# Rows of w_out in pairs, columns of the first layer two apart, and w_in's tile by quarters

## The chip, the cores and the metric

The kernel runs on one core of a Trainium2 chip. The metric is device time in microseconds of one execution; the median of three runs is compared. A profile of one execution shows each instruction of each engine: TensorE (PE, with its weight loads as PEld), VectorE (DVE), ScalarE (ACT), GpSimd (POOL), SyncE (SP), and the DMA queues.

## The reference

Forgetting attention for 8 batches of 8 heads (576 positions, 64 values a head), then a two-layer perceptron with a tanh GELU over the 4608 rows of 512 values that the heads make together.

```python
def _attn_ref(q, k, v, f):
    scores = scale * q @ k.T
    cum = np.cumsum(np.log(np.clip(f, 0.0001, 1.0)), axis=-1)
    scores = np.where(causal, -1e9, scores + cum[..., :, None] - cum[..., None, :])
    attn = softmax(scores)
    return attn @ v

def _moe_ref(x, w_in, w_out):          # x: 4608 x 512, w_in: 512 x 2048, w_out: 2048 x 512
    h = x @ w_in
    g = 0.5 * h * (1.0 + np.tanh(c * (h + 0.044715 * h * h * h)))
    return g @ w_out
```

Inputs and output are float32; the kernel computes its matmuls in bfloat16.

## The kernel before

**Work.** Attention goes in 16 groups of four heads (`scores`, `mask`, `denominators`, `attn_out`), whose results land transposed in `xT` (the 512 model values on partitions in four tiles `dt`, the rows along the tile). The perceptron goes in 9 chunks of 512 rows. Its first layer multiplies `w_in_sb` (loaded as weights, 128 columns at a time, one tile `ft` of 16 of the 2048 hidden values) with a piece of `xT` that streams through; the result has hidden values on partitions, and ScalarE's GELU writes it to `gT`. The second layer loads pieces of `gT` as weights and streams `w_out_sb`.

**First layer, three forms.** `mlp_in_half` (L436) and `mlp_in` (L400) multiply plainly. `unit` (L484) and `two_units` (L536) take a quarter u of the hidden values (512 columns) in a scheme of seven products in place of eight. For it `w_blocks` cuts the quarter in four blocks a11, a12, a21, a22: the first and second pair of `dt`, by the first and second 256 columns. `w_in_sums` (L466, L468) makes sums of them. For k = 3 it writes a21 in place: `a21 = a11 - a21`. The second layer has a scheme of the same kind (`weight_sums`, `seven_products`).

**Weight loads with a stride, before.** `scores` loads `kT`, whose tile keeps two values side by side, as every second element along the tile; `attn_out` loads `vw` as every second of 64 columns.

**Loads.** `w_in` (4 MB) and `w_out` (4 MB) are float32 in memory and bfloat16 on chip, so they go through GpSimd's queue, like q and k, and the early loads of v. `load_w_in(c)` brings one of eight pieces: 2 KB rows of memory become 1 KB on chip, two to a partition. `load_w_out(c)` brings four tiles of 128 rows, a row of memory (2 KB) to a partition.

**Order.** All is written out by hand: tables of short words (`FRONT`, `SECOND`, `STEADY`, `FLUSH`, `LAST`) that `run` turns into instructions in that order on each engine. `WI.c` and `WO.c` are the loads; `J`, `I`, `Q` and `E` are parts of the first layer; `F` of the second; `UW.u.k` is step k of `w_in_sums` for quarter u on VectorE. The framework adds the waits between engines: it notes which parts of a tile an instruction reads and writes and lets later ones that overlap wait. The last table has this stretch, in which the steps of quarter 1 are made while TensorE runs products of quarter 2 and the second layer (`e.1.u.n` is the next n products of unit u for the last chunk):

```python
F.0.4 F.0.3 UW.1.3 e.1.2.1 UW.1.4 e.1.1.1 F.0.5 e.1.1.2 F.0.5
```

Of the kernel before, what the change touches and what calls it, by code (L numbers as in the profile page):

```python
# [9 lines left out]
BF16 = mybir.dt.bfloat16  # L10
# [6 lines left out]
def kernel(  # L17
# [10 lines left out]
    nc = tc.nc  # L28
# [10 lines left out]
    N_DT = D_MODEL // 128  # L39
# [97 lines left out]
    gT = singles.tile([128, N_FT, CH], BF16, name="gT")  # L137
    g1, g2, g4 = many(3, [128, HF, HC], BF16, "gsum")
    u1, u2, u4 = many(3, [128, HF, HD], BF16, "usum")
    w_in_sb = singles.tile([128, N_DT, D_FF], BF16, name="w_in_sb")  # L140
    xsum = many(4, [128, 2, HC], BF16, "xsum")
    wsum = {u: many(3, [128, 2, HC], BF16, f"wsum{u}_") for u in UNIT_LIST}
    w_out_sb = singles.tile([128, N_FT, D_MODEL], BF16, name="w_out_sb")
# [43 lines left out]
        return ins  # L187

    w_in_hbm = moe_w_in.rearrange("(u p x) n -> p u x n", p=128, x=2)
    w_out_hbm = moe_w_out.rearrange("(t p) n -> p t n", p=128)  # L190

    def load_w_in(c):
        u, n = c % 2, D_FF // 4
        s = slice(n * (c // 2), n * (c // 2 + 1))
        return nc.gpsimd.dma_start(out=w_in_sb[:, 2 * u:2 * u + 2, s], in_=w_in_hbm[:, u, :, s])

    def load_w_out(c):
        n = N_FT // 4
        return nc.gpsimd.dma_start(out=w_out_sb[:, n * c:n * (c + 1), :],
                            in_=w_out_hbm[:, n * c:n * (c + 1), :])  # L200

    parts = [(0, QA), (QA, S)]

# [183 lines left out]
    def mlp_in(c, pr, spare=False):  # L387

        n0 = CH * c % RING
        spans = [(n0, CH)] if n0 + CH <= RING else [(n0, HC), ((n0 + HC) % RING, HC)]  # L390
        if spare:
            ph = psO.tile([128, 1024], FP32, name="ps_h", tag="po").rearrange("p (a n) -> p a n", n=512)
        else:
            ph = psS.tile([128, 2, 512], FP32, name="ps_h", tag="s")
        for dts in (range(N_DT - 1), range(N_DT - 1, N_DT)):
            for j in range(2):
                ft = 2 * pr + j
                for dt in dts:
                    for n, (h0, cols) in enumerate(spans):
                        nc.tensor.matmul(  # L400
                            ph[:, j, n * cols:(n + 1) * cols],
                            w_in_sb[:, dt, 128 * ft:128 * ft + 128],
                            xT[:, dt, h0:h0 + cols],
                            start=(dt == 0 and n == 0), stop=(dt == N_DT - 1),
                            skip_group_check=True,
                        )
                    if dt == N_DT - 1 and j == 1:
                        nc.scalar.activation(gelus(c, 2 * pr, 2), ph, AF.Gelu_apprx_tanh)  # L408
                    yield
# [11 lines left out]
    def mlp_in_half(half, g, spare=False):  # L421

        if spare:
            ph = psO.tile([128, 1024], FP32, name="ps_h", tag="po").rearrange("p (a n) -> p a n", n=512)
        else:
            ph = psS.tile([128, 2, 512], FP32, name="ps_h", tag="s")
        n0 = QA * half
        at = [ph.rearrange("p a (b n) -> p (a b) n", n=QA)]
        later[half, g] = lambda: nc.scalar.activation(gT[:, 4 * g:4 * g + 4, n0:n0 + QA], at[0], AF.Gelu_apprx_tanh)
        held[half, g] = at  # L430
        cut = 2 if spare else N_DT - 1
        for dts in (range(cut), range(cut, N_DT)):
            for j in range(4):
                ft = 4 * g + j
                for dt in dts:
                    nc.tensor.matmul(  # L436
                        ph[:, j // 2, QA * (j % 2):QA * (j % 2) + QA],
                        w_in_sb[:, dt, 128 * ft:128 * ft + 128],
                        xT[:, dt, n0:n0 + QA],
                        start=(dt == 0 and j % 2 == 0), stop=(dt == N_DT - 1),  # L440
                        skip_group_check=True,
                    )
                    if not spare and j == 3 and dt == N_DT - 1:
                        later[half, g]()
                    yield
# [9 lines left out]
        eng.tensor_sub(*((t1, b12, b11), (t2, b22, t1), (t3, b22, b12), (t4, b21, t2))[k - 1])  # L455

    def w_blocks(u):
        f1, f2 = slice(512 * u, 512 * u + 256), slice(512 * u + 256, 512 * u + 512)
        return w_in_sb[:, 0:2, f1], w_in_sb[:, 2:4, f1], w_in_sb[:, 0:2, f2], w_in_sb[:, 2:4, f2]

    def w_in_sums(u, k, eng):

# [7 lines left out]
    def unit(c, u, spare):  # L470

        a11, a12, s3, a22 = w_blocks(u)
        s1, s2, s4 = wsum[u]
        t1, t2, t3, t4 = xsum
        if spare:
            pa, pb = (psS.tile([128, 2, 512], FP32, name="ps_u", tag="s")[:, 0, :].rearrange("p (n t) -> p n t", t=HC)
                      for _ in range(2))
        else:
            pa, pb = (psM.tile([128, 2, HC], FP32, name="ps_u", tag="m") for _ in range(2))

        def multiply(ps, w, x, first):
            for n in range(2):
                for d in range(2):
                    nc.tensor.matmul(ps[:, n, :], w[:, d, 128 * n:128 * n + 128], x[:, d, :],  # L484
                                     start=(first and n == 0 and d == 0), stop=(d == 1), skip_group_check=True)

        def keep(ps, eng):
            t = unit_pool.tile([128, 2, HC], FP32, name="usnap", tag="usnap")
            if eng is nc.scalar:
                eng.copy(t, ps)  # L490
            else:
                eng.tensor_copy(t, ps)
            return t

        def result(a, t, src):
            ft = 4 * u + 2 * a
            nc.scalar.activation(gelus(c, ft, 2)[:, :, HC * t:HC * t + HC], src, AF.Gelu_apprx_tanh)

        def sum_of(a, t, ps, kept):
            nc.vector.tensor_add(kept, ps, kept)  # L500
            result(a, t, kept)

        multiply(pa, a11, x_block(c, 0, 0), True)
        p1 = keep(pa, nc.scalar)
        yield
        multiply(pb, a12, x_block(c, 1, 0), True)
        sum_of(0, 0, pb, p1)
        yield
        multiply(pa, s2, t2, False)
        v2 = keep(pa, nc.scalar)  # L510
        yield
        multiply(pb, s3, t3, True)
        p7 = keep(pb, nc.scalar)
        yield
        multiply(pa, s1, t1, False)
        sum_of(1, 1, pa, p7)
        yield
        multiply(pb, a22, t4, False)
        sum_of(1, 0, pb, v2)
        yield  # L520
        multiply(pa, s4, x_block(c, 1, 1), False)
        result(0, 1, pa)
        yield

    def two_units(c):

        blocks = [w_blocks(u) + tuple(wsum[u]) for u in (0, 2)]
        t1, t2, t3, t4 = xsum
        pa, pb = (psS.tile([128, 2, 512], FP32, name="ps_q", tag="s") for _ in range(2))

        def multiply(ps, which, x, first):
            for k in range(2):
                w = blocks[k][which]
                for n in range(2):
                    for d in range(2):
                        nc.tensor.matmul(ps[:, k, HC * n:HC * n + HC], w[:, d, 128 * n:128 * n + 128], x[:, d, :],  # L536
                                         start=(first and n == 0 and d == 0), stop=(d == 1), skip_group_check=True)
                if k == 0:
                    yield

        def keep(ps):
            t = unit_pool.tile([128, 2, 512], FP32, name="usnap", tag="usnap")
            nc.scalar.copy(t, ps)
            return t

        def result(a, t, src):
            nc.scalar.activation(  # L547
                gT.rearrange("p (u f) n -> p u f n", f=4)[:, 0:3:2, 2 * a:2 * a + 2, HC * t:HC * t + HC],
                src.rearrange("p u (f n) -> p u f n", n=HC), AF.Gelu_apprx_tanh)

        def sum_of(a, t, ps, kept):
            nc.vector.tensor_add(kept, ps, kept)  # L552
            result(a, t, kept)

        A11, A12, S3, A22, S1, S2, S4 = range(7)
        yield from multiply(pa, A11, x_block(c, 0, 0), True)
        p1 = keep(pa)
        yield
        yield from multiply(pb, A12, x_block(c, 1, 0), True)
        sum_of(0, 0, pb, p1)  # L560
        yield
        yield from multiply(pa, S2, t2, False)
        v2 = keep(pa)
        yield
        yield from multiply(pb, S3, t3, True)
        p7 = keep(pb)
        yield
        yield from multiply(pa, S1, t1, False)
        sum_of(1, 1, pa, p7)
        yield  # L570
        yield from multiply(pb, A22, t4, False)
        sum_of(1, 0, pb, v2)
        yield
        yield from multiply(pa, S4, x_block(c, 1, 1), False)
        result(0, 1, pa)
        yield
# [312 lines left out]
```

## Time and profile before

| | |
|---|---|
| median of three runs | 322.18 us (321.74 to 322.78) |
| profiled execution | 322.02 us, span 320.1 us |
| granted TensorE clock, mean | 1.000 |
| TensorE matmuls, busy | 311.8 us (97%) |
| TensorE weight loads, busy | 219.1 us (68%) |
| VectorE, ScalarE, GpSimd, busy | 242.5, 212.9, 109.9 us |
| `w_in` loads | 8, issued from 6.7 to 19.6 us |
| `w_out` loads | 4, issued from 21.4 to 29.7 us |

The span is the time from the first to the last instruction; the profiled execution's own time has some 2 us around it. A row of a group names line, engine, operation, tiles (out<-in), shapes and count, then busy time and the mean of one in ns, then idle time of the engine before them. A row of a timeline has start and length in us. Busy time of matmuls overlaps from one to the next, so their distance from start to start counts, not their length.

### The profile page before, as it was taken

How to read it: one execution, taken by the hardware profiler on the slowest of the kernel's cores; microseconds unless marked ns; L12 is line 12 of the kernel's file. 1: busy time of each engine (PE TensorE's matmuls, PEld its weight loads, DVE VectorE, ACT ScalarE, POOL GpSimd, SP SyncE). 2: the span in 40 equal slices, each digit the busy share in tenths (PEclk: the TensorE clock that was granted, in tenths of full speed). 3: DMA queues.
4: the chain of work that ended last, by engine and by line, in shares of the span. 5: the costliest groups of instructions: out<-in, count | busy, mean ns of one | idle time of the engine just before them, and what ended most of it. 6: DMA issues, size and time to landing. Idle time of an engine off the chain costs nothing.

```text
span 320.1 us, 11762 instructions
## 1 busy us (share of the span) xinstructions
PE 311.8 (97%) x5301; PEld 219.1 (68%) x5318; DVE 242.5 (76%) x369; ACT 212.9 (67%) x246; POOL 109.9 (34%) x148
## 2 busy tenths in 40 slices
PE   6899999999999999999999999999999999999996
PEld 2367734545676577776788878767776786688785
DVE  7667528598878889879877987699876865597674
ACT  3766885966766876877677866787686744836610
POOL 8799541830340417311850075206610140000000
PEclk9999999999999999999999999999999999999999
DMA  7999999985253901693149411961011110100203
GB/s 127 227 197 204 208 222 223 171 153 105 51 99 100 215 9 39 137 190 72 39 97 218 84 39 44 218 137 38 5 60 40 35 39 33 35 33 2 100 33 99
DMA packets 47491, 33.41 MB, mean 104 GB/s; under 512 B 29777, under 2 KB 42193, under 8 KB 47441
## 3 DMA queue, kind: packets, MB, share of 16 engines
q0 software_dynamic: 9632, 15.99, 29.1%
q1 hardware_dynamic: 37664, 16.60, 19.4%
q8 instruction: 41, 0.67, 0.9%
q14 instruction: 10, 0.07, 0.1%
q10 hardware_dynamic: 144, 0.07, 0.1%
HBM read 36.85 MB, written 9.44 MB: 145 GB/s over the span
## 4 chain that ended last, share of the span: by engine, by line
PE 91%; DMA 3%; ACT 2%; POOL 1%; DVE 1%; issue 1%; DVEq 0%; POOLq 0%
PE ps_w L616 30%; PE ps_h L400 19%; PE po L352 9%; PE ps_s L282 9%; PE ps_q L536 8%; PE pso L685 5%; PE ps_h L436 5%; PE ps_u L484 4%; DMA v_nat<-in_v_dram 3%; PE po_m L338 1%; ACT gT L408 1%; ACT pt L290 1%; POOL v_nat L183 0%; PE ps_o L352 0%; PE ps_p L616 0%
## 5 line engine op out<-in xcount | busy, mean ns | idle before, releaser
L290 ACT ACTIVATE pt<-ps_s 128x1024 bf16<-128x1024 f32 (+2 forms) x100 | 94.2, 991 | 38.1 <-PE ps_s L282 36.4
L296 POOL TENSOR_SCALAR_AFFINE_SELECT pt<-pt 128x512 bf16<-128x512 bf16 (+3 forms) x73 | 46.2, 643 | 96.6 <-ACT pt L290 73.7
L400 PE MATMUL ps_h<-xT,w_in_sb 128*128 128x512 bf16 (+1 forms) x308 | 65.6, 357 | 1.1 <-issue 0.3
L400 PEld LDWEIGHTS <-w_in_sb 128*128 128x128 bf16 x320 | 31.2, 98 | 26.6 <-issue 0.6
L408 ACT ACTIVATE gT<-ps_h 128x1024 bf16<-128x1024 f32 x34 | 34.6, 1018 | 20.3 <-PE ps_h L400 20.0
L616 PEld LDWEIGHTS <-gT 128*32 128x32 bf16 (+1 forms) x1171 | 44.1, 97 | 5.8 <-issue 2.4
L616 PE MATMUL ps_w<-w_out_sb,gT 128*32 128x256 bf16 (+1 forms) x996 | 42.5, 273 | 0.0
L616 PEld LDWEIGHTS <-gsum 128*32 128x32 bf16 (+1 forms) x903 | 35.3, 97 | 4.0 <-issue 1.5
L282 PE MATMUL ps_s<-qT,kT 32*128 32x64 bf16 (+5 forms) x896 | 35.4, 261 | 0.9 <-DVE qT L213 0.6
L552 DVE TENSOR_TENSOR usnap<-ps_q,usnap 128x1024 f32<-128x1024 f32 x15 | 17.9, 1222 | 18.5 <-PE ps_q L536 13.2
L616 PE MATMUL ps_w<-usum,gsum 128*32 128x256 bf16 (+1 forms) x749 | 30.1, 273 | 0.0
L282 PEld LDWEIGHTS <-kT 32*128 32x128 bf16 x896 | 16.4, 92 | 17.2 <-issue 10.2
L230 POOL TENSOR_TENSOR vw<-v_nat,wT 128x1280 bf16<-128x1280 f32 (+1 forms) x12 | 27.3, 2275 | 1.4 <-DMA v_nat<-in_v_dram 1.1
L633 DVE COPY snap<-ps_w 128x512 f32<-128x512 f32 x32 | 21.8, 681 | 6.6 <-PE ps_w L616 6.5
L213 DVE STREAM_TRANSPOSE kT<-k_c 128x576 f32<-128x576 f32 x16 | 19.4, 1243 | 7.0 <-DMA k_c<-in_k_dram 7.0
L547 ACT ACTIVATE gT<-usnap 128x1024 bf16<-128x1024 f32 x15 | 15.8, 1054 | 12.1 <-DVE usnap L552 11.7
L384 DVE TENSOR_TENSOR xT<-po,rb 128x576 bf16<-128x576 f32 x26 | 19.5, 751 | 5.1 <-PE po L352 4.9
L213 DVE STREAM_TRANSPOSE qT<-q_c 128x576 f32<-128x576 f32 x16 | 19.7, 1241 | 3.7 <-DMA q_c<-in_q_dram 3.7
L352 PE MATMUL po<-pt,vw 128*32 128x64 bf16 (+4 forms) x624 | 22.4, 278 | 0.0
L206 POOL DMA_DIRECT2D k_c<-in_k_dram x16 | 9.1, 567 | 34.9 <-DVE kT L213 23.0
L352 PEld LDWEIGHTS <-vw 128*32 128x32 bf16 x672 | 14.6, 97 | 9.3 <-issue 2.6
L536 PEld LDWEIGHTS <-w_in_sb 128*128 128x128 bf16 x160 | 15.7, 98 | 2.5 <-issue 0.4
(134 smaller groups left out, 481.4 us busy)
## 6 DMA issues: line engine op xcount, KB each, us to landing
out_dram<-o_st SPq DMA_DIRECT2D x35, 256.0 KB, 2.2
k_c<-in_k_dram POOLq DMA_DIRECT2D x16, 288.0 KB, 5.6
q_c<-in_q_dram POOLq DMA_DIRECT2D x16, 288.0 KB, 6.1
v_nat<-in_v_dram SPq DMA_DIRECT2D x16, 256.0 KB, 5.3
v_nat<-in_v_dram SPq DMA_DIRECT2D x20, 128.0 KB, 5.2
v_nat<-in_v_dram POOLq DMA_DIRECT2D x8, 256.0 KB, 8.8
w_in_sb<-in_moe_w_in_dram POOLq DMA_DIRECT2D x8, 256.0 KB, 7.9
w_out_sb<-in_moe_w_out_dram POOLq DMA_DIRECT2D x4, 512.0 KB, 9.8
```

What stands on the lines that cost most here:

```text
L213: return nc.vector.transpose(out=dst.rearrange("p s c -> p (s c)").bitcast(FP32) .rearrange("p (t a) -> p a t", a=n), in_=src.rearrange("p ...
L230: return eng.tensor_mul(vw[i % 2][:, t0:t1], vb[:, t0:t1, h0:h0 + 4, :], wT[:, i, t0:t1, :].unsqueeze(3).to_broadcast([128, t1 - t0, 4, D]))
L282: nc.tensor.matmul(tiles[h // 2][:, h % 2, c0:c0 + nq], key_columns(i, key, h, c), qq[32 * h:32 * h + 32, q0:q0 + nq, c], start=(c == 0 an ...
L290: nc.scalar.activation(p[:, 2 * g:2 * g + 2, off:off + n], t[:, :, 0:n], AF.Exp, scale=scale)
L296: nc.gpsimd.affine_select(out=x, in_=x, compare_op=ALU.is_ge, fill=0.0, base=0, pattern=pattern, channel_multiplier=-1)
L352: nc.tensor.matmul(po[r0:r0 + w.shape[-1], 448 + q0:448 + q0 + nq], w, p[:, h, col:col + nq], start=(key in (0, "low")), stop=(key in ("lo ...
L384: nc.vector.tensor_mul(xT[:, 2 * u + x, r0 + s0:r0 + s1], po, rbs[i, part])
L400: nc.tensor.matmul(ph[:, j, n * cols:(n + 1) * cols], w_in_sb[:, dt, 128 * ft:128 * ft + 128], xT[:, dt, h0:h0 + cols], start=(dt == 0 and ...
L408: nc.scalar.activation(gelus(c, 2 * pr, 2), ph, AF.Gelu_apprx_tanh)
L536: nc.tensor.matmul(ps[:, k, HC * n:HC * n + HC], w[:, d, 128 * n:128 * n + 128], x[:, d, :], start=(first and n == 0 and d == 0), stop=(d ...
L616: nc.tensor.matmul(ps[c0:c0 + width, n, cols[0]:cols[1]], x[:, j, 128 * n + c0:128 * n + c0 + width], w[:, j, cols[0]:cols[1]], start=(fir ...
L633: copy(kept[name], ps)
```

## The change

`w_out_hbm` is cut so that a partition takes two neighbouring rows of memory (4 KB, which are 2 KB on chip): tile 2t + x, partition p, now holds row 256t + 2p + x. So that the hidden values of `gT` stand on the same partitions, the first layer takes the columns of `w_in_sb` two apart: tile ft is every second column, from the odd or the even one, of a block of 256 (`ff_tile`, and `n:256:2` in the products). The tile of `w_in` is laid out by quarters of the hidden values, so that a quarter's four `dt` lie next to each other, 512 columns each. The tables are unchanged.

```diff
-    w_in_sb = singles.tile([128, N_DT, D_FF], BF16, name="w_in_sb")
+    w_in_sb = singles.tile([128, 4, N_DT, D_FF // 4], BF16, name="w_in_sb")
...
-    w_out_hbm = moe_w_out.rearrange("(t p) n -> p t n", p=128)
+    w_out_hbm = moe_w_out.rearrange("(t p x) n -> p t x n", p=128, x=2)
...
-        return nc.gpsimd.dma_start(out=w_in_sb[:, 2 * u:2 * u + 2, s], in_=w_in_hbm[:, u, :, s])
+        return nc.gpsimd.dma_start(out=w_in_sb[:, c // 2, 2 * u:2 * u + 2, :], in_=w_in_hbm[:, u, :, s])
 
     def load_w_out(c):
-        n = N_FT // 4
-        return nc.gpsimd.dma_start(out=w_out_sb[:, n * c:n * (c + 1), :],
-                            in_=w_out_hbm[:, n * c:n * (c + 1), :])
+        n = N_FT // 8
+        return nc.gpsimd.dma_start(
+            out=w_out_sb[:, 2 * n * c:2 * n * (c + 1), :].rearrange("p (t x) n -> p t (x n)", x=2),
+            in_=w_out_hbm[:, n * c:n * (c + 1)].rearrange("p t x n -> p t (x n)"))
+
+    def ff_tile(dt, ft):
+        n0 = 256 * (ft % 4 // 2)
+        return w_in_sb[:, ft // 4, dt, n0 + ft % 2:n0 + 256:2]
...
-                            w_in_sb[:, dt, 128 * ft:128 * ft + 128],      # mlp_in and mlp_in_half
+                            ff_tile(dt, ft),
...
     def w_blocks(u):
-        f1, f2 = slice(512 * u, 512 * u + 256), slice(512 * u + 256, 512 * u + 512)
-        return w_in_sb[:, 0:2, f1], w_in_sb[:, 2:4, f1], w_in_sb[:, 0:2, f2], w_in_sb[:, 2:4, f2]
+        w = w_in_sb[:, u]
+        return w[:, 0:2, 0:256], w[:, 2:4, 0:256], w[:, 0:2, 256:], w[:, 2:4, 256:]
...
-                    nc.tensor.matmul(ps[:, n, :], w[:, d, 128 * n:128 * n + 128], x[:, d, :],   # unit
+                    nc.tensor.matmul(ps[:, n, :], w[:, d, n:256:2], x[:, d, :],
...
-                        nc.tensor.matmul(ps[:, k, HC * n:HC * n + HC], w[:, d, 128 * n:128 * n + 128], x[:, d, :],   # two_units
+                        nc.tensor.matmul(ps[:, k, HC * n:HC * n + HC], w[:, d, n:256:2], x[:, d, :],
```

More of the change, by code (lines that the diff above doesn't have):

```diff
@@ L437, in mlp_in_half @@
                         ph[:, j // 2, QA * (j % 2):QA * (j % 2) + QA],
-                        w_in_sb[:, dt, 128 * ft:128 * ft + 128],
+                        ff_tile(dt, ft),
                         xT[:, dt, n0:n0 + QA],
```

## The prediction

> **What bounds the kernel now.** I read the page first (busy shares, chain of waits by engine and line), then the groups by line with shapes kept apart, then the timeline of the stretches that the change touches, then the DMA view of two early stretches.
>
> ```profile
> span 320.1 us, 11762 instructions
> ...
> PE 311.8 (97%) x5301; PEld 219.1 (68%) x5318; DVE 242.5 (76%) x369; ACT 212.9 (67%) x246; POOL 109.9 (34%) x148
> ...
> PE 91%; DMA 3%; ACT 2%; POOL 1%; DVE 1%; issue 1%; DVEq 0%; POOLq 0%
> PE ps_w L616 30%; PE ps_h L400 19%; PE po L352 9%; PE ps_s L282 9%; PE ps_q L536 8%; PE pso L685 5%; PE ps_h L436 5%; PE ps_u L484 4%; DMA v_nat<-in_v_dram 3%; PE po_m L338 1%; ACT gT L408 1%; ACT pt L290 1%; POOL v_nat L183 0%; PE ps_o L352 0%; PE ps_p L616 0%
> ```
>
> TensorE is the bound: 91% of the chain that ended last is matmuls, and 36% of the chain (L400, L536, L436, L484) is the first layer, whose weight loads this change rewrites. DMA is on the chain for 3% only, one early load of v. So an edit of loads from memory has little to win, and an edit of what feeds the matmuls has much to lose. The profiled execution took 322.02 us for a span of 320.1; the median of the three runs is 322.18, 0.16 above it.
>
> **Part 1, the columns with a stride of two.** 840 weight loads change: all 672 that read `w_in_sb` (rows below: 320 + 160 + 128 + 64) and 168 that read its sums in `unit` and `two_units`. Each still loads 128 columns; they lie 4 bytes apart now instead of 2.
>
> ```profile
> L400 PE MATMUL ps_h<-xT,w_in_sb 128*128 128x512 bf16 x244 | 57.9, 379 | 1.1 <-issue 0.3 <-ACT gT L408 0.2
> ...
> L400 PE MATMUL ps_h<-xT,w_in_sb 128*128 128x256 bf16 x64 | 7.6, 273 | 0.0
> ```
>
> ```profile
> L400 PEld LDWEIGHTS <-w_in_sb 128*128 128x128 bf16 x320 | 31.2, 98 | 26.6 <-issue 0.6
> L616 PEld LDWEIGHTS <-gT 128*32 128x32 bf16 x964 | 24.2, 97 | 1.5 <-issue 1.1
> ...
> L282 PEld LDWEIGHTS <-kT 32*128 32x128 bf16 x896 | 16.4, 92 | 17.2 <-issue 10.2 <-DVE qT L213 0.9 <-DVE gsum L594 0.8
> L536 PEld LDWEIGHTS <-w_in_sb 128*128 128x128 bf16 x160 | 15.7, 98 | 2.5 <-issue 0.4
> L352 PEld LDWEIGHTS <-vw 128*32 128x32 bf16 x672 | 14.6, 97 | 9.3 <-issue 2.6
> L436 PEld LDWEIGHTS <-w_in_sb 128*128 128x128 bf16 x128 | 12.1, 98 | 2.2 <-issue 0.4
> ...
> L484 PEld LDWEIGHTS <-w_in_sb 128*128 128x128 bf16 x64 | 6.3, 98 | 1.0
> ...
> L352 PEld LDWEIGHTS <-w_bf 128*1 128x1 bf16 x224 | 4.4, 84 | 3.4
> ```
>
> ```profile
> 117.83 0.35 PEld L282 LDWEIGHTS <-kT 32*128 32x128 bf16 x16 [0.21 <-issue]
> ```
>
> ```profile
> 205.56 1.75 PE ps_q L536 x16
> ```
>
> A load runs beside the matmul before it. In the chain, 16 matmuls of 256 columns took 1.75 us, 109 ns each; a load of 98 ns leaves 11 ns of that. Under 512 columns the slot is twice as long, so only loads under 256 columns matter: 64 + 128 + 160 + 64 = 416 of `w_in_sb`, and the 168 of the sums: 584.
>
> The trace already holds loads with this very stride. `kT` keeps pairs of values side by side and `scores` takes every second one: 128 columns, 4 bytes apart, half of them starting at the odd value, and they take 92 ns. The `vw` loads (every second of 64 columns, 128 rows) take the 97 ns that the contiguous `gT` loads of the same shape take. Sixteen `kT` loads went by in 0.35 us, four to each group of 32 rows: (0.35 - 0.092) / 3 = 86 ns from one to the next in a group, below 109. What no row shows is 128 columns with a stride over all 128 rows. Bounds: from below nothing (a strided read can't be shorter than a contiguous one of the same count); from above, one column takes 84 ns and 32 take 97, so 13 ns for 31 steps; the contiguous load of 128 columns takes 98, so it reads four at a step, and if the stride halved that it would need 32 steps more, 13 ns. I take 0, by the `kT` and `vw` rows, which are nearest in stride. The cover is the running matmul; where it is gone, at the first load of a run, 13 ns would show. The runs of the chain are of 8 matmuls or more but for a few, so 584 / 8 = 73 first loads, 0 to 0.9 us.
>
> **Part 2, a wait that the layout adds.** The two programs, built, have the same instructions in the same order on every engine; waits differ on TensorE only. Two weight loads of `w_in_sb` gain a wait for VectorE. In both, the load is the second one (d = 1) of the product with a11 (`w_blocks`), and it waits for the step of `w_in_sums` that overwrites a21 in place (k = 3, L468). These are different columns. But in the new tile a21 reaches from column 256 of d = 0 to column 1,023 of a quarter, across a11's second block at 512 to 767, and read with a stride that block is taken to overlap. The first is the product that opens the first `two_units`; the second is `e.1.1.1` in LAST (unit 1 of the last chunk).
>
> ```profile
> 128.70 0.42 DVE L468 TENSOR_TENSOR w_in_sb<-w_in_sb 128x512 bf16<-128x512 bf16 x1
> ```
>
> ```profile
> 131.30 0.93 PE L536 MATMUL ps_q<-xT,w_in_sb 128*128 128x256 bf16 x7
> ```
>
> ```profile
> 288.48 0.68 DVE L633 COPY snap<-ps_w 128x512 f32<-128x512 f32 x1
> ...
> 288.76 0.43 PEld L484 LDWEIGHTS <-w_in_sb 128*128 128x128 bf16 x4
> 288.86 0.60 PE L484 MATMUL ps_u<-xT,w_in_sb 128*128 128x256 bf16 x4
> 289.08 0.41 DVE L468 TENSOR_TENSOR v_nat<-v_nat,w_in_sb 128x512 bf16<-128x512 bf16 x1
> ...
> 289.30 0.71 PE L616 MATMUL ps_w<-w_out_sb,gT 128*128 128x256 bf16 x5
> 289.41 0.42 DVE L468 TENSOR_TENSOR w_in_sb<-w_in_sb 128x512 bf16<-128x512 bf16 x1
> ```
>
> ```profile
> 290.55 0.69 DVE L500 TENSOR_TENSOR usnap<-ps_u,usnap 128x512 f32<-128x512 f32 x1 [0.38 <-PE ps_u L484]
> ...
> 291.30 0.49 PE L484 MATMUL ps_u<-xsum,w_in_sb 128*128 128x256 bf16 x3
> ```
>
> ```profile
> 289.00:301.00 12.00, 12.00 (x112) 10.73 (x110) 7.71 (x15) 7.37 (x14) 0.00 (x0) 1.00 0.13 45
> 302.00:315.00 13.00, 13.00 (x109) 10.51 (x108) 9.23 (x14) 2.24 (x3) 0.00 (x0) 1.00 0.13 42
> ```
>
> The first wait is free: the in-place step ended at 128.70 + 0.42 = 129.12, and the product starts at 131.30. It would cost something only if VectorE came 2.1 us later.
>
> The second is not. The four loads of the product start at 288.76, one slot of 109 ns apart, so the second at 288.87. The step that it must now wait for runs from 289.41 to 289.83, with VectorE busy without a gap from 288.48, so it can't come sooner; and it waits for nothing that stands behind the stalled load, since its own inputs are done. From VectorE's end to TensorE's start takes 291.30 - 291.24 = 0.06 us (the pair at 290.55 and 291.30). So the load starts at 289.89: 1.02 us late. Queued behind it on TensorE, in order: the other three matmuls of the product, the five L616 matmuls at 289.30 and all the rest of the last stage. That stage has no hole to give the time back: TensorE is busy 12.00 of 12.00 us and 13.00 of 13.00 in the two windows (columns: length, then PE busy). The L500 step at 290.55, which had waited 0.38 us for TensorE, just waits longer. The stall reaches the end whole: **+1.02 us**. Bounds: 0.9, if the restart saves a part of the usual 0.1 from load to matmul, and 1.1, if the first load after a wait shows 0.1 of its 98 ns.
>
> **Part 3, the loads from memory.** `load_w_out` issues the same four DMAs on POOL, each with 256 pieces of 2 KB on chip instead of 512 of 1 KB. `load_w_in` keeps its pieces; only their places change.
>
> ```profile
> 26.00:28.00 2.00, 2.00 (x34) 1.43 (x33) 1.96 (x4) 1.99 (x2) 2.00 (x3) 1.00 1.21 199
> 32.50:34.50 2.00, 2.00 (x21) 1.79 (x20) 0.00 (x0) 1.90 (x6) 1.34 (x2) 1.00 1.09 204
> ```
>
> ```profile
> q0 software_dynamic: 391, 0.40, 121.0%
> ```
>
> ```profile
> q0 software_dynamic: 205, 0.41, 109.4%
> ```
>
> ```profile
> L195 POOL DMA_DIRECT2D w_in_sb<-in_moe_w_in_dram x8: 704/716/722, 6.7 to 19.6; - x8
> ```
>
> ```profile
> L199 POOL DMA_DIRECT2D w_out_sb<-in_moe_w_out_dram x4: 772/777/785, 21.4 to 29.7; - x4
> ...
> DMA to landing us min/median/max: 8.3/9.8/12.6
> ```
>
> ```profile
> 29.74 8.84 PE ps_h L436 x80
> 38.58 1.41 PE pso L685 x21
> ...
> 43.57 2.27 PE pso L685 x33
> ```
>
> From 26 to 28 us the queue moved 391 packets of about 1 KB (the weights), 199 GB/s; from 32.5 to 34.5 it moved 205 of about 2 KB on average (q and k), 204 GB/s. The rate goes by bytes, not by pieces. The 2 MB of w_out take 10.5 us at 199 and 10.3 at 204: 0.26 us won over all four loads. POOL saves 777 - 716 = 61 ns an issue (256 pieces against 512), 0.24 us in all. Neither is on the path: the last load, issued at 29.7, lands by 29.7 + 12.6 = 42.3, and the last quarter of its first use falls in the run at 43.57; before it TensorE is full (80 matmuls in 8.84 us, 110 ns each). Cost 0; between -0.5 and 0.
>
> The DMA page of the Trainium skill ("DMA: Bandwidth & Descriptors", Why small descriptors are slow) puts about 3 cycles of fixed cost on a packet beside one per 32 bytes: 35 for 1 KB and 67 for 2 KB, an estimate of 4% or 0.45 us on w_out. By that rule the load gains a little more than by the rows, and the sum would be the same, as it is hidden.
>
> **Sum.** 322.02 + 1.02 + 0 + 0 = 323.04 against the profiled execution; on the median of the runs, 322.18 + 1.02 = **323.2 us**. About 0.3% is what a measurement of this kernel can tell from no change, 0.97 us: the stall sits just above that line, and of the terms that I left at 0, the one that is not all hidden (first loads, 0 to 0.9) adds.
>
> **The rivals.**
> - *The strided load over 128 rows is slower and shows.* At 13 ns more it would be 111 + 11 = 122 ns against 109, 13 ns on each of 584 loads: 7.6 us, 330.8 with the stall. It decides from 11 ns more per load. Against it: the 92 ns of `kT`, and 86 ns from load to load. The TensorE page of the Trainium skill ("TensorE: Matmul & The Clock Gate", LDWEIGHTS) gives P / 1.2 for a plain load, 107 ns at 128 columns; with the 11 ns that is 9 over the slot, some 5 us, by an estimate from its figure. The same page's section on weight-path modes says that the four-wide read works packed or strided, which the `kT` row bears out.
> - *The other side, faster: the early stage shortens.* The software queue is first in, first out, and the k, q and v loads behind w_out land sooner; if VectorE's and POOL's steps on them set TensorE's pace there, 0.5 us of loads and issue come off, and more if a piece of 2 KB takes much less than two of 1 KB. It shows as faster from 1.02 + 0.97 = 2.0 us on: 321.2 at most. That is a fifth of the 10.5 us that w_out takes, all of it on the path. Against it: equal rates, and the runs of L436 without a hole from 29.74.
> - *No effect: the stall does not come,* because VectorE reaches the step 1 us sooner in this run, or TensorE later: 322.2. For it: only that both clocks are near each other; against it the unbroken VectorE row from 288.48.
>
> **How the numbers follow.** The stall alone: 0.60, of it 0.44 above the line of 0.3% and 0.16 below it. Slower loads: 0.15. Faster early stage: 0.12, of it 0.09 past 0.3% and 0.03 within. No effect: 0.13. Slower 0.44 + 0.15 = 0.59; same 0.16 + 0.03 + 0.13 = 0.32; faster 0.09. The range runs from 321.6 (no effect with the early 0.5 won) to 325.0 (stall, first loads, and a small share of 2 to 3 ns on 584 loads); it leaves out most of the slower loads and part of the faster case.
>
> **What would show it.** Right: a hole of 0.9 to 1.1 us on TensorE in the product `e.1.1.1`, put down to VectorE's in-place step, nothing else longer; strided loads at 92 to 100 ns with 109 ns from matmul to matmul; w_out issues near 716 ns; the same landings within 0.5 us. Wrong: matmuls of the first layer more than 110 ns apart; no hole near 289 us; a chain whose early part has changed.

## The result and the profile after

The changed kernel took 323.37 us in the median of 19 runs (322.34 to 324.06), the kernel before 322.32 in as many (321.48 to 323.64). The ratio is 1.0029, with a 95% interval of 1.0018 to 1.0040: slower by 0.93 us, 0.6 to 1.3. The profiled execution took 323.74 us. Two executions of the kernel with the step moved ahead took 531 and 1113 us, far from all others, and are left out of its ratio.

The timeline of the stretch around `e.1.1.1` in the changed kernel (start, length, engine, line, operation, tiles, and in brackets the idle time before and who ended it; L474, L490, L506 and L622 are L468, L484, L500 and L616 of before):

```profile
289.62 0.10 PEld L490 LDWEIGHTS <-w_in_sb 128*128 128x128 bf16 x1
289.73 0.27 PE L490 MATMUL ps_u<-xT,w_in_sb 128*128 128x256 bf16 x1
...
290.28 0.41 DVE L474 TENSOR_TENSOR w_in_sb<-w_in_sb 128x512 bf16<-128x512 bf16 x1
...
290.75 0.22 PEld L490 LDWEIGHTS <-w_in_sb 128*128 128x128 bf16 x3 [1.03 <-DVE w_in_sb L474]
290.75 0.50 PE L490 MATMUL ps_u<-xT,w_in_sb 128*128 128x256 bf16 x3 [0.75 <-DVE w_in_sb L474]
...
291.09 0.71 PE L622 MATMUL ps_w<-w_out_sb,gT 128*128 128x256 bf16 x5
...
292.34 0.69 DVE L506 TENSOR_TENSOR usnap<-ps_u,usnap 128x512 f32<-128x512 f32 x1 [1.31 <-PE ps_u L490]
```

What was one run of four loads and four matmuls is now one and three. The second load should have come a slot after the first, at 289.62 + 0.11 = 289.73; it came at 290.75, 1.02 us late, 0.06 after VectorE's in-place step ended (290.28 + 0.41 = 290.69). The L622 matmuls follow the start of the product by 291.09 - 289.62 = 1.47 us; before, the same two points lay 289.30 - 288.76 = 0.54 apart. So the work behind the wait is 0.93 us late. VectorE's L506 waits 1.31 us for TensorE in place of 0.38: the same 0.93. The difference of 0.09 between 1.02 and 0.93 is won at the restart: there the load and its matmul both start at 290.75, where 0.11 lies between the two in the run (289.62 and 289.73). In the view of waits for 280 to 319 us the two rows of the step are the only new ones of any size:

```profile
PEld L490 <- DVE w_in_sb L474: 1.0, 1, 1.0
...
PE ps_u L490 <- DVE w_in_sb L474: 0.8, 1, 0.8
```

The groups by line, weight loads of `w_in_sb` alone, all with the stride now:

```profile
L406 PEld LDWEIGHTS <-w_in_sb 128*128 128x128 bf16 x320 | 31.2, 98 | 26.5 <-issue 0.6
L542 PEld LDWEIGHTS <-w_in_sb 128*128 128x128 bf16 x160 | 15.6, 98 | 2.5 <-issue 0.4
L442 PEld LDWEIGHTS <-w_in_sb 128*128 128x128 bf16 x128 | 12.0, 98 | 2.6 <-issue 0.4 <-DMA w_in_sb<-in_moe_w_in_dram 0.4
L490 PEld LDWEIGHTS <-w_in_sb 128*128 128x128 bf16 x64 | 6.2, 98 | 2.0 <-DVE w_in_sb L474 1.0
```

98 ns in each, as before. Three rows of the chain of waits of the changed kernel (start, length, what), and then its w_out issues and the software queue:

```profile
12.72 7.57 DMA w_in_sb<-in_moe_w_in_dram
...
30.59 8.84 PE ps_h L442 x80
...
206.41 1.75 PE ps_q L542 x16
```

```profile
L199 POOL DMA_DIRECT2D w_out_sb<-in_moe_w_out_dram x4: 713/726/750, 22.0 to 30.1; - x4
```

```profile
q0 software_dynamic: 8608, 15.99, 28.1%
```

The queue moves 1,024 packets fewer than before (9,632), 256 for each of the four w_out loads. The runs of 80 and of 16 matmuls take 8.84 and 1.75 us, to the hundredth what they took before; both begin 0.85 us later (30.59 against 29.74, 206.41 against 205.56). That 0.85 has arisen ahead of 30 us and doesn't grow; 1.79 at the end is 0.85 and the 0.93 of the stall. One by one, the weight loads of the two profiles keep a distance of 0.81 to 0.86 us from 33 to 288 us. The early 0.85 isn't the change's, as the experiments show. The span is 321.9 for 320.1.

### The profile page after: what moved, and what is told of

Read it like the earlier page. It is cut to its first block, busy times and chain, and to the rows that moved or that the text cites. A ratio compares the mean times of both kernels' runs of the same rounds, so it can differ in the third digit from the quotient of the medians.

```text
span 321.9 us, 11779 instructions
## 1 busy us (share of the span) xinstructions
PE 314.6 (98%) x5318; PEld 219.3 (68%) x5318; DVE 243.2 (76%) x369; ACT 212.9 (66%) x246; POOL 108.7 (34%) x148
## 4 chain that ended last, share of the span: by engine, by line
PE 90%; DMA 3%; ACT 3%; DVE 2%; POOL 0%; issue 0%; DVEq 0%
PE ps_w L622 29%; PE ps_h L406 19%; PE po L358 9%; PE ps_s L288 9%; PE ps_q L542 8%; PE pso L691 5%; PE ps_h L442 4%; PE ps_u L490 4%; DMA w_in_sb<-in_moe_w_in_dram 2%; ACT pt L296 1%; PE po_m L344 1%; DMA f_all<-in_f_dram 1%; ACT gT L414 1%; PE ps_o L358 0%; PE ps_p L622 0%; PE idle_ps L261 0%
## 5 line engine op out<-in xcount | busy, mean ns | idle before, releaser
L302 POOL TENSOR_SCALAR_AFFINE_SELECT pt<-pt 128x512 bf16<-128x512 bf16 (+3 forms) x73 | 45.2, 629 | 98.4 <-ACT pt L296 75.5
L406 PE MATMUL ps_h<-xT,w_in_sb 128*128 128x512 bf16 (+1 forms) x320 | 66.9, 358 | 0.2 <-ACT gT L414 0.2
L622 PEld LDWEIGHTS <-gT 128*32 128x32 bf16 (+1 forms) x1171 | 44.1, 97 | 5.8 <-issue 2.4
L622 PE MATMUL ps_w<-w_out_sb,gT 128*32 128x256 bf16 (+1 forms) x996 | 42.5, 273 | 0.0
L622 PEld LDWEIGHTS <-gsum 128*32 128x32 bf16 (+1 forms) x903 | 35.3, 97 | 4.0 <-issue 1.5
L622 PE MATMUL ps_w<-usum,gsum 128*32 128x256 bf16 (+1 forms) x749 | 30.1, 273 | 0.0
## 6 DMA issues: line engine op xcount, KB each, us to landing
w_out_sb<-in_moe_w_out_dram POOLq DMA_DIRECT2D x4, 512.0 KB, 10.1
```

What stands on the lines that cost most here:

```text
L302: nc.gpsimd.affine_select(out=x, in_=x, compare_op=ALU.is_ge, fill=0.0, base=0, pattern=pattern, channel_multiplier=-1)
L406: nc.tensor.matmul(ph[:, j, n * cols:(n + 1) * cols], ff_tile(dt, ft), xT[:, dt, h0:h0 + cols], start=(dt == 0 and n == 0), stop=(dt == N_ ...
L622: nc.tensor.matmul(ps[c0:c0 + width, n, cols[0]:cols[1]], x[:, j, 128 * n + c0:128 * n + c0 + width], w[:, j, cols[0]:cols[1]], start=(fir ...
```

## The experiments

Ratios are to the kernel before, run beside it on the same chip. "Late" below is the distance of a weight load from the same load in the profile of before; where it steps, time was lost or won.

**The wait alone, in the kernel before** (nothing else of the change):

```diff
-            eng.tensor_sub(*(...)[k - 2])
+            steps[u, k] = eng.tensor_sub(*(...)[k - 2])
...
+                    if late is not None and n == 0 and d == 1:
+                        after(ins, late)                       # wait for that step
...
-        multiply(pa, a11, x_block(c, 0, 0), True)
+        multiply(pa, a11, x_block(c, 0, 0), True, steps[1, 3] if u == 1 else None)
```

> The kernel before, with nothing but the one wait added: the second weight load of the product with a11 of unit 1 in the last chunk waits for the in-place step of a21. Contiguous columns, old tile, old loads. Theory: a hole of 0.9 to 1.0 us on TensorE near 289 us, 323.2 to 323.4 us, ratio 1.003, the same as the whole change. Rival: the hole is there but is worth less than half, ratio 1.000 to 1.0015.

Measured: 323.09 us, ratio 1.0019 (1.0009 to 1.0029). Its timeline:

```profile
288.74 0.10 PEld L486 LDWEIGHTS <-w_in_sb 128*128 128x128 bf16 x1
...
289.39 0.42 DVE L470 TENSOR_TENSOR w_in_sb<-w_in_sb 128x512 bf16<-128x512 bf16 x1
...
289.86 0.22 PEld L486 LDWEIGHTS <-w_in_sb 128*128 128x128 bf16 x3 [1.03 <-DVE w_in_sb L470]
...
290.21 0.71 PE L620 MATMUL ps_w<-w_out_sb,gT 128*128 128x256 bf16 x5
```

The same hole: 290.21 - 288.74 = 1.47 us, as in the changed kernel. The loads are 0.02 to 0.03 us early from 73 to 288 us and 0.91 late from there to the end. The ratio lies between the two expectations, and its interval just reaches the 0.29% of the stall; what decides for the theory is the trace.

**The change without the wait.** The in-place step is made in two, one for each d. No load with a stride then spans columns that a step writes, and TensorE waits for the same as before, instruction by instruction.

```diff
-            eng.tensor_sub(*((s2, s1, a11), (a21, a11, a21), (s4, a12, s2))[k - 2])
+            for out, in0, in1 in {2: [(s2, s1, a11)], 3: [(a21[:, d], a11[:, d], a21[:, d]) for d in range(2)],
+                                  4: [(s4, a12, s2)]}[k]:
+                eng.tensor_sub(out, in0, in1)
```

> The changed kernel whole, but the in-place step of w_in_sums (k = 3) made as two instructions, one for each d. Then no load with a stride spans columns that a step writes, and TensorE's waits are those of the kernel before, one for one. Theory (the one wait is all that the change costs): the hole of 0.93 us at 289 us is gone, and since 128x512 takes 0.42 us and 128x1024 0.69, half of 128x512 should take 0.28: 0.14 us more of VectorE for each of three steps, under cover; time 322.2 to 322.6, ratio 0.9995 to 1.001. Rival (a part of the cost lies elsewhere in the change: strided loads, w_out by pairs, the tile by quarters): ratio stays at 1.002 to 1.004.

Measured: 322.06 us beside 322.50 for the kernel before, ratio 0.9992 (0.9982 to 1.0002).

```profile
288.08 0.42 PEld L492 LDWEIGHTS <-w_in_sb 128*128 128x128 bf16 x4
...
288.62 0.71 PE L624 MATMUL ps_w<-w_out_sb,gT 128*128 128x256 bf16 x5
288.74 0.49 DVE L476 TENSOR_TENSOR w_in_sb<-w_in_sb 128x256 bf16<-128x256 bf16 x2
...
289.88 0.69 DVE L508 TENSOR_TENSOR usnap<-ps_u,usnap 128x512 f32<-128x512 f32 x1 [0.32 <-PE ps_u L492]
```

The four loads are one run again and the second layer follows 0.54 us after them, although the step comes later than the loads, as it may. The two halves take 0.49 us for 0.42, less than expected. From 33 us to the end the loads stay 0.67 to 0.72 us ahead of before: no time is lost anywhere behind the start. So strided loads, pairs of rows and the quarters together cost nothing that these runs can tell (the interval ends at 1.0002), and the 0.29% is the wait.

**The parts alone, in the kernel before.** First the tile by quarters with plain columns; then w_out by pairs with plain columns.

```diff
-    w_in_sb = singles.tile([128, N_DT, D_FF], BF16, name="w_in_sb")
+    w_in_sb = singles.tile([128, 4, N_DT, D_FF // 4], BF16, name="w_in_sb")
...
-                            w_in_sb[:, dt, 128 * ft:128 * ft + 128],
+                            w_in_sb[:, ft // 4, dt, 128 * (ft % 4):128 * (ft % 4) + 128],
```

> The kernel before with w_in's tile by quarters and nothing else: contiguous columns, rows of w_out one by one. Its waits are those of before. Theory: 322.3 us, ratio 1.000 (0.999 to 1.001). Rival: if the new places of w_in slow the early loads or the sums made of them, up to the 0.8 us that the first 20 us of the changed kernel's profile were late, ratio 1.001 to 1.0025.

```diff
-    w_out_hbm = moe_w_out.rearrange("(t p) n -> p t n", p=128)
+    w_out_hbm = moe_w_out.rearrange("(t p x) n -> p t x n", p=128, x=2)      # and load_w_out as in the change
```

> The kernel before with w_out loaded in pairs of rows and nothing else; the first layer's columns are not matched to it, so the second layer multiplies rows of w_out in another order and the output is not the reference's. Same instructions and waits as before. Theory: the four loads take 0.2 us less in all and POOL 0.2 us less, both hidden: ratio 1.000 (0.999 to 1.001). Rival (the early stage hangs on these loads): 0.3 to 0.5 us less, ratio 0.9985 to 0.999.

Measured: 322.21 us, 0.9990 (0.9976 to 1.0005), and 322.30 us, 0.9995 (0.9985 to 1.0005). Neither has a hole at 289 us. The quarters alone don't bring the wait, and the pairs win nothing alone. The profile of the pairs alone loses time at another place, 0.47 us at 51 us, as its chain of waits shows:

```profile
36.50 12.64 DMA v_nat<-in_v_dram
...
49.26 1.49 DVE vw L231
50.76 0.35 DVE pt L327
...
51.14 0.61 PE po L353 x16
```

A load of v that GpSimd issues behind w_out lands at 49.14, VectorE makes `vw` of it and then masks `pt`, and attention on TensorE waits for that. Apart from the change on the old tile, three profiles with pairs lose 0.28 to 0.47 us there (this one, the step moved ahead and the early loads reordered) and three lose nothing (the change itself, the step in two, ten matmuls ahead); the three with single rows lose nothing. Whether the pairs have a part in it is not shown; the ratio of 0.9995 gives them no cost.

**The loads by themselves.** Behind the work of the kernel before, eight stretches of 64 matmuls, for 32, 64, 128 and 256 columns first with plain loads and then with a stride of two:

```diff
+            nc.tensor.matmul(ps[:, 0:cols], w_in_sb[:, j % N_DT, c0:c0 + 128 * step:step], xT[:, j % N_DT, 0:cols], ...)
...
+        for cols in (32, 64, 128, 256):
+            for step in (1, 2):
+                loads(step, cols)
```

> The kernel before with eight stretches of 64 plain matmuls added at the end, into a free bank: weights of 128 columns over all 128 rows of w_in_sb, contiguous and two apart, each under 32, 64, 128 and 256 streamed columns. Theory (a strided load takes no longer, or stays hidden): under 256 and 128 columns the distance from matmul to matmul is the same for both strides, 109 and 56 ns; weight loads read 98 ns, or up to 111 for the strided. Rival: the strided one is over 109 ns apart under 256 columns, or over 60 under 128. What a load takes by itself shows under 32 and 64 columns.

The timeline of the weight loads, 64 columns with the stride, 128 plain and strided, 256 plain and strided, and then the line's loads together (shortest, median and longest in ns):

```profile
323.18 1.93 PEld L858 LDWEIGHTS <-w_in_sb 128*128 128x128 bf16 x64 [0.15 <-issue]
325.26 3.61 PEld L858 LDWEIGHTS <-w_in_sb 128*128 128x128 bf16 x64 [0.15 <-issue]
329.05 3.61 PEld L858 LDWEIGHTS <-w_in_sb 128*128 128x128 bf16 x64 [0.18 <-issue]
332.84 6.97 PEld L858 LDWEIGHTS <-w_in_sb 128*128 128x128 bf16 x64 [0.18 <-issue]
340.04 6.86 PEld L858 LDWEIGHTS <-w_in_sb 128*128 128x128 bf16 x63 [0.23 <-issue]
```

```profile
L858 PEld LDWEIGHTS <-w_in_sb x512: 95/98/98, 317.4 to 346.8; 128*128 128x128 bf16 x171
```

In this one execution all 512 loads take 95 to 98 ns, with the stride or without. Under 128 columns 64 loads start within (3.61 - 0.10) / 63 = 56 ns of each other in both forms; under 256, (6.97 - 0.10) / 63 = 109 and (6.86 - 0.10) / 62 = 109. Under 64 columns it is 29 with the stride, and under 32 the median distance of the starts is 25 ns for both. So a load over 128 rows can start 25 ns after the one before it, while that one still runs: its 98 ns are not the pace of loads. Part 1's price of a strided load, 0, holds far below the 109 ns that this kernel needs.

**The step moved ahead** (`UW.1.3` right behind `UW.1.1`, some 10 us earlier), run twice in the changed kernel:

```diff
-        T.1.2 UW.1.1 i.0.7.4 ...
-        F.0.4 F.0.3 UW.1.3 e.1.2.1 ...
+        T.1.2 UW.1.1 UW.1.3 i.0.7.4 ...
+        F.0.4 F.0.3 e.1.2.1 ...
```

> The changed kernel with one word of the last table moved: the in-place step of quarter 1 (UW.1.3) stands right behind UW.1.1, about 9 us before the product that now waits for it. Theory (the stall is the whole difference): no hole on TensorE in e.1.1.1, 1.0 us less than the changed kernel, so 322.3 us and a ratio to before of 1.000 (0.999 to 1.001). Rival (the strided loads or the new places of w_in in the early stage cost the difference, spread out, and the hole is given back elsewhere): the hole goes but 0.5 us or more stays, a ratio of 1.0015 to 1.003.

> The same kernel as in the first experiment (the changed kernel with UW.1.3 right behind UW.1.1), run again for an undisturbed profile and a closer interval. Theory: no hole on TensorE in e.1.1.1, every instruction from 27 us to the end at a constant distance from the kernel before, ratio 1.000 (0.999 to 1.001). Rival: 0.5 us or more is left, ratio 1.0015 or more.

Measured: ratio 1.0000 (0.9987 to 1.0012), and 1.0005 (0.9992 to 1.0018). The profile of the second run shows the hole gone at 289 us and a smaller one at 284.8:

```profile
284.07 0.69 DVE L602 TENSOR_TENSOR gsum<-gsum,gT 128x1024 bf16<-128x1024 bf16 x1
...
284.82 0.39 PE L622 MATMUL ps_w<-usum,gsum 128*128 128x256 bf16 x2 [0.25 <-DVE gsum L602]
```

VectorE has no slack there: 0.4 us put in ahead makes its sum for the second layer late, and TensorE waits for that. The loads go from 0.06 us early to 0.34 late, 0.40 lost for 0.93 won. So the ratios agree with the theory, but this trace is not that of a kernel without any wait; the step made in two is.

**Ten matmuls moved ahead** of the product, the wait left in:

```diff
-        ... UW.1.4 e.1.1.1 F.0.5 e.1.1.2 F.0.5 e.1.1.1 ...
+        ... UW.1.4 F.0.5 F.0.5 e.1.1.1 e.1.1.2 e.1.1.1 ...
```

> The changed kernel, with ten matmuls of the second layer put ahead of the product e.1.1.1 in the order of the last stage; the wait stays. Theory (a wait costs only what no other work covers): the ten take 1.09 us, so the product's second load comes 0.07 us after the step's end and the hole at 289 us is gone; against that the copy of ps_w on VectorE ended 0.3 us after the first of the ten would start, so up to 0.3 us of another wait may come, and VectorE's addition for the product comes 1.1 us later; ratio 0.9995 to 1.0015. Rival (the order has no slack, what is moved ahead waits for as long as the product did): ratio 1.002 to 1.004.

Measured: 322.98 us, ratio 1.0017 (1.0005 to 1.0030), between the two expectations; the 0.71 us that its trace loses, 0.22%, is the rival's number.

```profile
289.26 0.42 DVE L474 TENSOR_TENSOR w_in_sb<-w_in_sb 128x512 bf16<-128x512 bf16 x1
289.58 0.38 PE L622 MATMUL ps_w<-usum,gsum 128*128 128x256 bf16 x2
...
289.80 1.04 PE L490 MATMUL ps_u<-xT,w_in_sb 128*128 128x256 bf16 x8
...
290.49 0.58 ACT L496 COPY usnap<-ps_u 128x512 f32<-128x512 f32 x1 [0.93 <-PE ps_u L490]
...
291.13 0.60 PE L490 MATMUL ps_u<-xsum,v_nat 128*128 128x256 bf16 x4 [0.29 <-ACT usnap L496]
```

The wait itself is covered: the product runs without a break from 289.80. But the products now stand close together, and the third must wait until ScalarE has copied the first out of the accumulator that it writes. VectorE's addition waits for the same copy, and the fourth product for the addition. The loads are 0.15 us early at 287 and 0.56 late at 294: 0.71 lost. My theory's bound, that only VectorE's copy and addition could come in the way, left ScalarE out.

**The change on the old tile** (stride and pairs, but `w_in_sb` as before):

```diff
-    w_in_sb = singles.tile([128, 4, N_DT, D_FF // 4], BF16, name="w_in_sb")
+    w_in_sb = singles.tile([128, N_DT, D_FF], BF16, name="w_in_sb")
...
-        return w_in_sb[:, ft // 4, dt, n0 + ft % 2:n0 + 256:2]                 # n0 of the quarter
+        return w_in_sb[:, dt, n0 + ft % 2:n0 + 256:2]                          # n0 of the tile
```

> The changed kernel with w_in's tile left as before (one row of 2048 hidden values per d), so that only the stride and the pairs of w_out stay. Built, its first products wait for loads whose columns they do not read: the loads of d = 1 of quarter 0 for WI.2 and WI.6, of d = 3 for WI.3, WI.4 and WI.7, which land up to 27.5 us where the products stand at 19 to 22; the two waits for the in-place step stay. Theory (a stride makes the framework take a whole stretch as read; waits are the price of this change): TensorE stands some 6 us before 28 us, 4 to 7 us more than the changed kernel, 327 to 331 us, ratio 1.013 to 1.027. Rival (these waits are covered by other work, as most are): within 1 us of the changed kernel, ratio 1.000 to 1.006.

Measured: 335.05 us, ratio 1.0392 (1.0368 to 1.0416), 12.6 us over the kernel before and 11.7 over the changed one, where 4 to 7 over the changed one were expected. Rows of its timeline, TensorE and GpSimd:

```profile
20.87 0.82 PE L442 MATMUL ps_h<-xT,w_in_sb 128*128 128x256 bf16 x3 [2.98 <-DMA w_in_sb<-in_moe_w_in_dram]
...
29.95 2.53 PE L442 MATMUL ps_h<-xT,w_in_sb 128*128 128x256 bf16 x11 [5.77 <-DMA w_in_sb<-in_moe_w_in_dram]
```

```profile
21.99 2.13 POOL L195 DMA_DIRECT2D w_in_sb<-in_moe_w_in_dram  x3 [3.50 <-PE ps_h L442]
```

On the old tile a piece of `w_in` goes to two `dt` that lie 2,048 columns apart, so its span takes in the columns of other quarters. A strided load of an odd `dt` waits for pieces that it doesn't read (the load of `dt` 0 went at 17.61 us, the one of `dt` 1 behind it waited until 20.87), and, which I had not counted, GpSimd's next load from memory waits 3.50 us until TensorE has read what the load doesn't write. The queue behind it shifts as a whole, and from 53 us on the loads are 12 us late. Not all of that is waiting: the two waits make the loads 3.2 and 6.2 us later, and another 2.6 are lost between and behind them, where the granted clock is 0.50 (third number from the end of this row of a stretch) and the matmuls take longer:

```profile
20.00:33.50 13.50, 6.86 (x67) 3.60 (x71) 1.75 (x3) 1.53 (x3) 4.73 (x7) 0.50 0.78 141
```

The eleven matmuls at 29.95 took 2.53 us, some 230 ns each, where 109 is usual. The step of 0.93 at 288 us is there too, so the stride brings the false wait on the old tile as on the new one. The layout by quarters pays for itself: with the stride it saves 12 us and leaves that one wait.

**The early loads reordered**, in the changed kernel with the step moved ahead:

```diff
-        ... B.1.512 WI.5 B.1.512 ... WI.1 WI.2 B.1.128 ... H.0.2.0 WI.3 H.0.1.0 W.0 LP.2 ...
+        ... B.1.512 WI.1 B.1.512 ... WI.2 LP.2 B.1.128 ... H.0.2.0 WI.5 H.0.1.0 W.0 WI.3 ...
```

> The changed kernel with UW.1.3 right behind UW.1.1 and, in the first table, the loads put by first use: WI.1 where WI.5 stood, then WI.2, the v piece LP.2, WI.5, WI.3. In the changed kernel's profile the start hung on WI.1 (issued behind two masks on POOL, landed 20.29), in another one on LP.2 (23.28). Theory (TensorE is full from 30 us on, and the start is the only other place that moves): the start's late cases go, 0.2 to 1.0 us less than the kernel before, ratio 0.997 to 0.9995. Rival (the start hangs on the first k and q loads and on the clock of the first matmuls, whatever comes behind): ratio 1.000.

Measured: 322.65 us, ratio 1.0009 (0.9994 to 1.0024). A miss: the order of the early loads brings nothing.

**The early 0.85 us.** In the kernels whose order is that of the changed kernel up to 280 us, the distance from before at 73 us is +0.85 (the change itself), -0.06 (step moved), -0.17 (ten ahead) and -0.68 (step in two); the quarters alone, without stride or pairs, have +1.26. It differs from profile to profile of the same early order. The timeline of TensorE at the start, of the changed kernel and then of the one with the step in two:

```profile
7.47 0.83 PE L267 MATMUL idle_ps<-kT,idle 128*128 128x512 bf16 x2
...
9.09 0.82 PE L288 MATMUL ps_s<-qT,kT 32*128 32x256 bf16 x16
```

```profile
7.38 0.59 PE L267 MATMUL idle_ps<-kT,idle 128*128 128x512 bf16 x2
...
8.50 0.52 PE L288 MATMUL ps_s<-qT,kT 32*128 32x256 bf16 x16
```

The same sixteen matmuls take 0.82 us in one and 0.52 in the other, and start 0.59 us apart. From 8 to 9 us the granted clock (third number from the end) was half in the first, full in the second:

```profile
8.00:9.00 1.00, 1.00 (x3) 0.15 (x1) 0.72 (x1) 0.00 (x0) 1.00 (x2) 0.50 1.08 191
```

```profile
8.00:9.00 1.00, 0.90 (x19) 0.43 (x18) 0.45 (x1) 0.00 (x0) 0.97 (x2) 1.00 1.07 175
```

The first scores came later, and with them GpSimd's masks and the loads queued behind those. The quarters alone were late in the same way: the two idle matmuls of L267 (L261 there) took 1.06 us, though that profile gives a clock of 1.00 at the time. What decides it was not looked for.

## Why the prediction was right

**The sum.** 323.2 was forecast and 323.37 measured, with the stall as the only term. Part 2 named the load, the step, the instruction queue behind it and the end: the load was 1.02 us late as worked out, and the work behind it 0.93, near the lower bound of 0.9 that the restart was said to be able to reach. So the price taken was 0.09 too large. The difference of the two medians, 1.05, agrees better with 1.02 than it should: 0.93 is the stall, and the rest is the scatter of the start, which moves a single execution by a microsecond. The measured 0.29% lies just under the 0.3% at which the prediction parted slower from same, so it came out on the side that had 0.32, of it 0.16 for the stall; with 19 runs of each kernel the interval still keeps it clear of no change. The upper end of the range, 325.0, doesn't follow from its terms: 323.2 + 0.9 and 2 to 3 ns on 584 loads make 325.3 to 325.9. Nothing hangs on that.

**That it reaches the end whole** held in the changed kernel and in the wait alone, to 0.01 us. **That the first new wait is free** held: no load shifts near 131 us. **That the stall is the one cost** is shown from both sides, by adding it alone and by taking it out alone. **That the layout adds the wait** was put too narrowly: the quarters without the stride don't have it, and the stride on the old tile does, so it is the stride that brings it.

**Part 1** held: 98 ns as before, 109 from matmul to matmul, and the 0 to 0.9 us allowed for first loads came out at nothing. The rival of slower loads is out. But the margin was read wrongly: Part 1 left 11 ns between a load of 98 and the slot of 109, and the rival's 7.6 us rest on the same sum, whereas loads that can start every 25 ns leave some 80 ns. By an estimate from these distances, 13 ns more would have been hidden under 256 columns as well. The rival had the TensorE page of the Trainium skill ("TensorE: Matmul & The Clock Gate", LDWEIGHTS) beside it, with 107 ns for 128 columns; the loads issued every 25 ns don't agree with that as a limit on their rate.

**Part 3** held in size. Back to back on the queue, the third and fourth w_out land 2.57 us apart by rows (28.93 + 10.75 and 29.67 + 12.58 in the profile of before) and 2.49 by pairs (29.45 + 11.03 and 30.15 + 12.82): 0.08 for each load against 0.065 forecast, a quarter of 0.26. The DMA page of the Trainium skill ("DMA: Bandwidth & Descriptors", Why small descriptors are slow) gave an estimate of 4% by its fixed cost on a packet; the trace, with 3%, is near it. GpSimd's issue took 726 ns, not 716. The median landing, 10.1 us against 9.8, follows the queue ahead of the load, which scatters more than that. In the change it is all hidden, and the rival of a faster early stage is out with it: the pairs alone gave 0.9995. The cover is thinner than Part 3 says: in three other profiles TensorE waits at 51 us for work on a v load from that queue.

**A test that would have misled.** I had named a chain whose early part has changed as a sign that the prediction is wrong. It did change, from a load of v to one of `w_in`, and by 0.85 us; but the same early order gives 0.85 or -0.68 there. A comparison of single profiles has to set that stage apart before it says anything.

## What to carry to other kernels

Weight loads with a stride of two cost TensorE nothing here, but an access with a stride covers a span, and a framework that compares spans sees overlaps that aren't there: look for instructions that gained a wait, on the loading queue as well as on TensorE, before pricing any transfer. Lay a tile out so that what is loaded, overwritten and read together is contiguous; where one span still crosses another, cutting the writer in two (0.07 us more of VectorE, at a place where it waits 0.3 us for TensorE) removed what moving work around only exchanged for other waits. On an engine that is full to the end, as here, a stall of 0.93 us is 0.93 us at the end, whereas a transfer that lands under cover is worth nothing.

## What the hardware showed that I had not expected

- A weight load of 128 by 128 takes 98 ns but can follow the one before it after 25 ns (under 32 streamed columns), with the columns next to each other or two apart.
- Two halves of a 128x512 VectorE subtraction in bfloat16 took 0.49 us in the last stage, against 0.41 to 0.42 for the whole: each 287 ns by itself on average, with some of it overlapping.
- Profiles of kernels with the same early order lie from 0.68 us ahead of the kernel before to 0.85 behind it at 73 us, most of it from TensorE's first 15 us, and keep that distance to 280 us. In the late one the granted clock was half from 8 to 10 us.
